# One power on GpSimd for both units of a step, the first tile's decoding behind it, and larger costs in the planner

## The chip, the cores and the metric

The kernel runs on one core of a Trainium2 chip. The core has a matrix engine (TensorE, PE in the rows), three engines for elementwise work (VectorE as DVE, ScalarE as ACT, GpSimd as POOL) and a queue engine (SyncE, SP) that issues most of the transfers. Each engine runs its own list of instructions in order and waits on semaphores for the others. The metric is the device time of one execution in microseconds, lower is better. It is compared with that of the kernel before on the same chip.

## The reference, cut to what matters

Three stages follow one another: a chunked linear-attention scan, a gated feed-forward layer behind an RMS norm, and a feed-forward layer with a squared ReLU.

```python
# scan, per chunk: M = (C B^T) * decay;  y = M x + (C state) * decay;  state = decay_full * state + sum(B x)
x = attn_out.transpose(0, 2, 1, 3).reshape(B * S, H * D)          # 3072 tokens of 256
rms = np.sqrt(np.mean(x * x, axis=-1, keepdims=True) + 1e-06)
xn = x / rms * rms_g
g = xn @ w_gate;  val = xn @ w_val                                # 256 -> 1536
x = (g * sigmoid(g) * val) @ w_out                                # 1536 -> 256
r = np.maximum(x @ w_in, 0.0)                                     # 256 -> 2048
out = (s * (r * r) + b) @ w_out2                                  # 2048 -> 256
```

The factor 1/rms is the part that the change touches: the kernel takes it as (mean of squares + 1e-6) to the power -0.5, on GpSimd.

## The kernel before

**The scan** goes in 16 steps of two *units* (`NPAIR = 2`, `NUNIT = 32`); a unit is one chunk of 48 positions of two batches. The stages of a step are `scan` (decay products `ab`, then a scan into `a_sb`), `gram` (64 small products `y<-raw_bc`, and the masks `m` from them on VectorE), `outs` (`y<-m,xh`, copied to `yt` by ScalarE), `back` (four transposes `y<-ident,yt` that put tokens on partitions, then the RMS norm) and `turn` (four transposes `y<-ident,xn` and the copies to `xth`, `xtl`, the input of the first layer). In `back`, for each unit: the state rows go to `xh` of the next step (`keep_state`), ScalarE squares the tokens with a running sum (`xn,ss<-y`, an ACTIVATE and a read of its accumulator), VectorE adds 1e-6 (`ss<-ss`), GpSimd takes the power (`rs<-ss,fixed`, a 128x1 tensor_tensor) and ScalarE scales the tokens (`xn<-y,rs`).

**The two layers** go over 8 blocks of 384 tokens, two steps each. The weights come as 64-bit floats and are decoded on the chip (`decode`: VectorE masks `e<-raw` and `raw<-raw`, ScalarE `e<-e` and `sg<-raw`, VectorE `w1f<-raw`, `e<-e,sg`, `w1f<-w1f,e`). Block 0 of layer 1 runs in halves of 192 columns with four-pass f32 products straight from `w1f` (`hidden1_plain`: four `h<-xth,w1f`, a SiLU on ScalarE, a product `h<-h,h` on VectorE, two `o<-h,w1f`), since the weights of tile m have only just been decoded. All later products are split into three one-pass products of a high and a low part, 384 columns each. Layers 1 and 2 of the blocks alternate, and the later scan steps are laid between their products.

**The order** on every engine is written by the class `Plan`, which records every operation and issues all of them from its method `issue` (one line, so every row of the trace has that line, L343 before and L349 now). It is a list scheduler: `price` gives the cost of an operation, `need` the delay from an operation to one that depends on it (a semaphore), `forward` and `backward` make the order from these. So a changed price moves instructions on all engines. `paced` operations are the products of the two layers; a *bundle* holds the products of one stage of both units of a step together, from unit 4 (`FREE`) on. Before `issue`, small bf16 products on constants are put in where the plan has TensorE idle at the start. `nc.after` makes the operations that follow wait, in the plan alone, for a recorded one.

Of the kernel before, what the change touches and what calls it, by code (L numbers as in the profile page):

```python
# [8 lines left out]
F32 = mybir.dt.float32  # L9
F32R = mybir.dt.float32r  # L10
# [6 lines left out]
AF = mybir.ActivationFunctionType  # L17
ALU = mybir.AluOpType

P = 128  # L20
# [8 lines left out]
NPAIR = 2  # L29
NUNIT = CPB * NPAIR  # L30
NCLIP = 2 * NPAIR
FREE = 2 * NPAIR
# [8 lines left out]
DM = 256  # L41
# [4 lines left out]
class Engine:  # L46
    def __init__(self, plan, name):
        self.plan, self.name = plan, name
# [5 lines left out]
class Plan:  # L54
# [16 lines left out]
    EARLY = 18.0  # L71
    STICK = 0.03
    SWITCH = {"matmul": 0.24, "transpose": 0.15}
    PASSES = 3

    def __init__(self, nc):
        self.nc, self.ops, self.clock, self.pace = nc, [], 0.0, False
        self.seen, self.rings, self.masks, self.before, self.heads = {}, {}, {}, {}, {}
        self.closed, self.sent, self.turns, self.bundle = set(), None, False, None
        self.fresh, self.after = False, None  # L80
        for e in ("tensor", "vector", "scalar", "gpsimd", "sync"):
            setattr(self, e, Engine(self, e))

    def add(self, eng, fn, args, kw):
# [21 lines left out]
        if self.fresh and op["eng"] == "tensor":  # L106
            op["dur"] += self.SWITCH[fn]
            self.fresh = False
# [72 lines left out]
    def need(self, op, o):  # L181
        if o is not op:
            lag = 0.0 if o["eng"] == op["eng"] == "tensor" else self.SEM_OF.get(o["eng"], self.SEM)
            op["preds"][o["i"]] = lag + (self.DMA_TAIL if o["fn"] == "dma_start" else 0.0)

    def price(self, eng, fn, args, kw):
        out = kw.get("out", args[0] if args else None)
        n = out.free_size()
        aps = [a for a in list(args) + list(kw.values()) if hasattr(a, "tensor")]
        psum = any("PSUM" in str(a.space) for a in aps)  # L190
        if fn == "dma_start":
            return max(0.06, out.nbytes() / self.DMA_RATE)
        if eng == "tensor":
            if fn == "transpose":
                return max(n / 1.2, 80) / 1e3 + 0.005
            w, four = kw["lhsT"], kw["lhsT"].dtype == F32
            cols = w.free_size()
            if w.ap[0][1] <= R:
                return 0.030 if w.ap[0][1] == NST else 0.014
            return max(4 * n / 2.4 + 5 if four else n / 2.285 + 7, (1.64 if four else 0.8) * cols) / 1e3  # L200
        if eng == "scalar":
            extra = 93 * sum(k in kw and hasattr(kw[k], "tensor") for k in ("scale", "bias"))
            extra += 230 if "accum_out" in kw else 120 if out.ap[0][1] < 32 else 0
            return (n / 1.2 + (60 if psum else 100) + extra) / 1e3
        if eng == "vector":
            sizes = [SIZE[a.dtype] for a in aps if a.free_size() > 1]
            fast = not psum and fn in ("tensor_scalar", "tensor_copy", "memset")
            fast = fast or (fn == "tensor_tensor" and not psum and max(sizes) == 2)
            more = 62 if fn == "scalar_tensor_tensor" and hasattr(kw["scalar"], "tensor") else 0
            if fn == "tensor_tensor_scan":  # L210
                n *= 2
            return (n / (1.92 if fast else 0.96) + 67 + more) / 1e3
        if fn == "tensor_tensor":
            return 0.7
        return n / 1.15e3 + (0.25 if fn == "affine_select" else 0.06)

    def lasts(self, op, now):
# [91 lines left out]
    def issue(self, idle, warm):  # L309
# [13 lines left out]
        found = []  # L323
        for _ in range(self.PASSES):
            start, stop = self.forward(succs, late)
# [31 lines left out]
def scan_glu_relu2(ctx: ExitStack, tc: tile.TileContext, bc, xr, aa, cst, w1, w2, gn, sv, bv, out):  # L357
    nc = Plan(tc.nc)
    PS = bass.MemoryType.PSUM

    const = ctx.enter_context(tc.tile_pool(name="const", bufs=1))
# [5 lines left out]
    att2 = ctx.enter_context(tc.tile_pool(name="att2", bufs=2))  # L367
# [17 lines left out]
    mhalf, emin = fixed[:, 0:1], fixed[:, 1:2]  # L385
    a_cl = const.tile([P, 4, R], F32, name="a_cl")
    warm = const.tile([P, 1], F32, name="warm")
    a_scr = dram.tile([2 * NUNIT, NH * AW], F32, name="a_scr")

    w1h = [wts.tile([P, 6, P], F32R, name=f"w1h{m}") for m in range(F1)]  # L390
# [6 lines left out]
    a_t, x_t, m_t, y_t, yt_t, xn_t = {}, {}, {}, {}, {}, {}  # L397
# [67 lines left out]
    def bundled(name, units, products):  # L465
        if units[0] >= FREE:
            nc.bundle = f"{name}{units[0]}"
        nc.fresh = True
        for c in units:
            products(c)  # L470
            nc.fresh = nc.fresh or units[0] < FREE
        nc.bundle = None
# [62 lines left out]
    def keep_state(c, tok):  # L535
        for z in range(2):
            rows = slice(z * R, z * R + NST)
            copy = nc.scalar.copy if c >= NPAIR else nc.vector.tensor_copy
            copy(out=x_t[c + NPAIR][rows], in_=tok[rows])

    def back(units):
        bundled("b", units, back_products)
        if units[0] == 0:
            nc.first_back = len(nc.ops) - 1
        for c in units:
            tok = y_t[c][:, 0, 0:DM]
            if c + NPAIR < NUNIT:
                keep_state(c, tok)
            xn = att2.tile([P, DM], F32, tag="xn", name="xn")
            ss = att2.tile([P, 1], F32, tag="ss", name="ss")  # L550
            nc.scalar.activation(out=xn, in_=tok, func=AF.Square, scale=DM ** -0.5, accum_out=ss)
            rs = att2.tile([P, 1], F32, tag="rs", name="rs")
            nc.vector.tensor_scalar(out=ss, in0=ss, scalar1=1e-6, scalar2=None, op0=ALU.add)
            nc.gpsimd.tensor_tensor(out=rs, in0=ss, in1=mhalf, op=ALU.pow)
            nc.scalar.activation(out=xn, in_=tok, func=AF.Copy, scale=rs)
            xn_t[c] = xn


    def columns(t, j):
# [30 lines left out]
    def stream():  # L590
        s = []
        for c in range(0, NUNIT, NPAIR):
            units = range(c, c + NPAIR)
            s += [(6 * c + t, units, f) for t, f in zip((2, 4, 8, 11, 14), (scan, gram, outs, back, turn))]
        s.sort(key=lambda e: e[0])
        return [(units, f) for _, units, f in s]


    def decode(raw, out, n):

        low = raw.bitcast(U32).rearrange("p (n w) -> p n w", w=2)[:, :, 0]
        high = raw.bitcast(I32).rearrange("p (n w) -> p n w", w=2)[:, :, 1]
        top_u = raw.bitcast(U16).rearrange("p (n w) -> p n w", w=4)[:, :, 3]
        top_i = raw.bitcast(I16).rearrange("p (n w) -> p n w", w=4)[:, :, 3]
        e = dec_p.tile([P, 6 * P], U16, tag="e", name="e")[:, :n]
        sg = dec_p.tile([P, 6 * P], BF16, tag="sg", name="sg")[:, :n]

        nc.vector.tensor_scalar(out=e, in0=top_u, scalar1=0x7FF0, scalar2=None, op0=ALU.bitwise_and)
        nc.scalar.activation(out=e, in_=e, func=AF.Relu, scale=8.0, bias=emin)
        nc.scalar.activation(out=sg, in_=top_i, func=AF.Sign)  # L610

        nc.vector.tensor_scalar(
            out=high, in0=high, scalar1=0xFFFFF, scalar2=0x100000,
            op0=ALU.bitwise_and, op1=ALU.bitwise_or,
        )
        nc.vector.scalar_tensor_tensor(
            out=out, in0=low, scalar=2.0 ** -32, in1=high, op0=ALU.mult, op1=ALU.add
        )
        pw = e.bitcast(BF16)
        nc.vector.tensor_tensor(out=pw, in0=pw, in1=sg, op=ALU.mult)  # L620
        nc.vector.tensor_tensor(out=out, in0=out, in1=pw, op=ALU.mult)

# [14 lines left out]
    def decode1(m):  # L637
        if m not in raw1:
            load1(m)
        raw = raw1.pop(m)  # L640
        w1f[m] = wlo.tile([P, 6, P], F32, tag="wlo", name="w1f")
        decode(raw, flat(w1f[m]), 6 * P)
# [10 lines left out]
    def decode2(m):  # L653
        raw = w2_p.tile([P, 4 * P], I64, tag="w2", name="raw2")
        words(raw, w2[m])
        w2f[m] = raw.bitcast(F32).rearrange("p (n w) -> p n w", w=2)[:, :, 1]
        decode(raw, w2f[m], 4 * P)
# [125 lines left out]
    def drain(n):  # L783
        while len(pending) > n:
# [4 lines left out]
                      in_=aa.rearrange("c (u f) -> (c u) f", u=2))  # L789
# [7 lines left out]
        out=ident, in_=ident, compare_op=ALU.not_equal, fill=1.0, base=0,  # L797
# [3 lines left out]
    for z in range(2):  # L801
        rows = slice(z * R, (z + 1) * R)
        nc.vector.tensor_copy(
            out=delta[rows, :, 0:CH], in_=ident[rows, None, z * R + NST:(z + 1) * R].to_broadcast([R, NH, CH])
        )
        nc.vector.memset(delta[z * R:z * R + NST, :, 0:1], 1.0)
    for u in range(4):
        rows = slice(u * 32, (u + 1) * 32)
        nc.vector.tensor_copy(
            out=raw_bc[rows, :, 0:NST], in_=ident[rows, None, u * 32:u * 32 + NST].to_broadcast([32, SLOTS, NST])  # L810
# [136 lines left out]
```

## Time and profile before

| | us |
|---|---|
| median of 3 runs | 668.23 |
| lowest and highest | 666.39, 670.76 |
| the profiled execution's own time | 669.25 |
| its span in the trace | 667.1 |
| TensorE busy in the span | 649.6 |
| VectorE busy | 385.2 |
| ScalarE busy | 361.4 |
| GpSimd busy | 36.0 |

The span is what the trace covers; the profiled execution took 2.15 us more than it. Busy times are sums over the span: an engine that is busy for half of it may still be the one that is waited for in one stretch.

### The profile page before, as it was taken

To read this page: it belongs to the slowest core of one execution; us is meant where nothing else is said; L and a number is where in the kernel's file an instruction comes from. 1 tells how busy PE (TensorE), PEld (TensorE's weight loads), DVE (VectorE), ACT (ScalarE), POOL (GpSimd) and SP (SyncE) were. 2 spreads that over 40 slices of the span, in tenths; PEclk is the share of its full clock that TensorE was granted. 3 is DMA by queue.
4 is the path that set the end of the run, shared out by engine and by line. 5 is a ranking of instruction groups with operands and counts; after the bars stand their busy time and mean duration, and the time that the engine had idled before them with its cause. 6 is when DMAs were issued, how large, how long until landed. Compare 5 with 4: busy or idle time off the path is not lost.

```text
span 667.1 us, 14004 instructions
## 1 busy us (share of the span) xinstructions
PE 649.6 (97%) x5575; PEld 629.8 (94%) x5575; DVE 385.2 (58%) x832; ACT 361.4 (54%) x814; POOL 36.0 (5%) x76
## 2 busy tenths in 40 slices
PE   6899999999999999999999999999999999999997
PEld 4699899899999999999999989999999999999997
DVE  6799999899644553355534464344633554344443
ACT  3688748876545663357534573346533565344453
POOL 3000200100000000001000010000000000000000
PEclk9699999999999999999999999999999999999999
DMA  7587660400001040003100030000400000000000
GB/s 216 183 250 267 199 240 13 93 1 0 1 2 25 23 96 13 0 2 84 46 0 1 14 93 25 1 1 13 93 25 0 1 3 25 0 1 1 11 13 25
DMA packets 26176, 35.06 MB, mean 53 GB/s; under 512 B 13696, under 2 KB 20480, under 8 KB 26112
## 3 DMA queue, kind: packets, MB, share of 16 engines
q1 hardware_dynamic: 25856, 33.98, 17.5%
q8 instruction: 44, 0.72, 0.4%
q10 hardware_dynamic: 256, 0.20, 0.1%
q14 instruction: 20, 0.16, 0.1%
HBM read 30.92 MB, written 3.25 MB: 51 GB/s over the span
## 4 chain that ended last, share of the span: by engine, by line
PE 87%; DVE 4%; ACT 3%; POOL 2%; issue 1%; DMA 1%; SPq 0%; DVEq 0%; POOLq 0%
PE h L343 48%; PE o L343 33%; PE y L343 6%; POOL rs L343 2%; ACT s L343 1%; DVE w1f L343 1%; DVE e L343 1%; DMA a_sb<-a_scr 1%; PE ab L343 1%; ACT xh L343 1%; DVE m L343 0%; DVE raw L343 0%; ACT xn L343 0%; ACT e L343 0%; DMA xh<-in_xr 0%
## 5 line engine op out<-in xcount | busy, mean ns | idle before, releaser
L343 ACT ACTIVATE s<-h 128x384 f32<-128x384 f32 x212 | 104.1, 491 | 152.5 <-PE h L343 110.3
L343 PE MATMUL h<-x,w2hl 128*128 128x384 f32 x768 | 165.4, 341 | 0.0
L343 DVE TENSOR_TENSOR lo<-s,hi 128x384 fp32r<-128x384 f32 x212 | 118.0, 556 | 48.3 <-ACT hi L343 37.3
L343 PEld LDWEIGHTS h<-x,w2hl 128*128 128x128 f32 x768 | 135.4, 188 | 1.1
L343 PE MATMUL o<-hi,w2hl 128*128 128x384 f32 (+1 forms) x512 | 133.0, 338 | 0.0
L343 PE MATMUL h<-xth,w1h 128*128 128x384 f32 x336 | 114.2, 340 | 0.3 <-ACT xth L343 0.3
L343 PE MATMUL h<-xtl,w1h 128*128 128x384 f32 x336 | 113.8, 340 | 0.0
L343 PE MATMUL h<-xth,w1l 128*128 128x384 f32 x336 | 113.5, 338 | 0.0
L343 DVE CAST hi<-s 128x384 fp32r<-128x384 f32 x128 | 46.0, 359 | 113.8 <-ACT s L343 103.2
L343 PEld LDWEIGHTS o<-hi,w2hl 128*128 128x128 f32 x512 | 93.2, 188 | 0.5
L343 DVE TENSOR_TENSOR s<-h,s 128x384 f32<-128x384 f32 x84 | 46.6, 555 | 78.0 <-PE h L343 78.0
L343 PE MATMUL o<-lo,w2hl 128*128 128x384 f32 (+1 forms) x256 | 86.6, 338 | 0.0
L343 ACT CAST hi<-s 128x384 fp32r<-128x384 f32 x84 | 43.1, 513 | 74.6 <-DVE s L343 74.4
L343 ACT ACTIVATE s<-s 128x384 f32<-128x384 f32 x128 | 67.3, 526 | 3.4
L343 PEld LDWEIGHTS h<-xth,w1h 128*128 128x128 f32 x336 | 63.1, 188 | 1.2 <-ACT xth L343 0.6
L343 PEld LDWEIGHTS h<-xtl,w1h 128*128 128x128 f32 x336 | 63.1, 188 | 0.5 <-DVE xtl L343 0.4
L343 PEld LDWEIGHTS h<-xth,w1l 128*128 128x128 f32 x336 | 63.1, 188 | 0.0
L343 PE MATMUL o<-hi,w1l 128*128 128x384 f32 x168 | 57.0, 339 | 0.0
L343 PE MATMUL o<-hi,w1h 128*128 128x384 f32 x168 | 56.9, 339 | 0.0
L343 PE MATMUL o<-lo,w1h 128*128 128x384 f32 x168 | 56.6, 337 | 0.0
L343 POOL TENSOR_TENSOR rs<-ss,fixed 128x1 f32<-128x1 f32 x32 | 30.6, 986 | 447.1 <-DVE ss L343 447.1
L343 PEld LDWEIGHTS o<-lo,w2hl 128*128 128x128 f32 x256 | 48.1, 188 | 0.0
(66 smaller groups left out, 698.2 us busy)
## 6 DMA issues: line engine op xcount, KB each, us to landing
raw<-in_w SPq DMA_DIRECT2D x12, 768.0 KB, 4.9
raw<-in_w SPq DMA_DIRECT2D x16, 512.0 KB, 5.8
a_sb<-a_scr SPq DMA_DIRECT2D x28, 196.0 KB, 4.1
raw_bc<-in_bc SPq DMA_DIRECT2D x64, 64.0 KB, 3.4
xh<-in_xr SPq DMA_DIRECT2D x60, 48.0 KB, 2.9
out_t<-ob SPq DMA_DIRECT2D x14, 192.0 KB, 2.5
out_t<-ob SPq DMA_DIRECT2D x4, 96.0 KB, 2.4
xh<-in_xr ACTq DMA_DIRECT2D x4, 48.0 KB, 3.6
```

The lines of the kernel that those rows point to most:

```text
L343: getattr(engine, op["fn"])(*op["args"], **op["kw"])
```

## The change

Of a step, both units' sums of squares now stand in one tile `ss` of two columns. One `ss<-ss` and one power `rs<-ss,fixed`, both 128x2, follow the squares of both units, where two of each stood before; the two `xn<-y,rs` come behind. In the first step the result of the power is copied on VectorE to a tile `held` that nothing reads, and the first tile's `w1f<-raw` is placed behind that copy in the plan; the first tile's `e<-e` on ScalarE is placed behind the squares. In the planner a power costs 0.9 us in steps below unit 4 and 2.0 us after (0.7 before), the products of a bundle count 0.6 us more on what they wait for on other engines, and a product of layer 1 counts 1.0 us more on `xth` and `xtl`.

```diff
+    LATE = 0.6
@@ def need
+            if op["eng"] == "tensor" != o["eng"] and self.bundle is not None:
+                lag += self.LATE
+            if op["paced"] and str(getattr(o["kw"].get("out"), "name", "")).startswith("xt") and op["kw"]["rhs"].dtype == F32R:
+                lag += 1.0
@@ def price
         if fn == "tensor_tensor":
-            return 0.7
+            return 0.9 if self.now_free else 2.0
@@ def back
+        ss = att2.tile([P, NPAIR], F32, tag="ss", name="ss")
...
-            xn = att2.tile([P, DM], F32, tag="xn", name="xn")
-            ss = att2.tile([P, 1], F32, tag="ss", name="ss")
-            nc.scalar.activation(out=xn, in_=tok, func=AF.Square, scale=DM ** -0.5, accum_out=ss)
-            rs = att2.tile([P, 1], F32, tag="rs", name="rs")
-            nc.vector.tensor_scalar(out=ss, in0=ss, scalar1=1e-6, scalar2=None, op0=ALU.add)
-            nc.gpsimd.tensor_tensor(out=rs, in0=ss, in1=mhalf, op=ALU.pow)
-            nc.scalar.activation(out=xn, in_=tok, func=AF.Copy, scale=rs)
-            xn_t[c] = xn
+            xn = xn_t[c] = att2.tile([P, DM], F32, tag="xn", name="xn")
+            nc.scalar.activation(
+                out=xn, in_=tok, func=AF.Square, scale=DM ** -0.5, accum_out=ss[:, c % NPAIR:c % NPAIR + 1]
+            )
+        if units[0] == 0:
+            nc.squares = len(nc.ops) - 1
+        rs = att2.tile([P, NPAIR], F32, tag="rs", name="rs")
+        nc.now_free = units[0] < FREE
+        nc.vector.tensor_scalar(out=ss, in0=ss, scalar1=1e-6, scalar2=None, op0=ALU.add)
+        nc.gpsimd.tensor_tensor(out=rs, in0=ss, in1=mhalf.to_broadcast([P, NPAIR]), op=ALU.pow)
+        if units[0] == 0:
+
+            nc.vector.tensor_copy(out=held, in_=rs)
+            nc.held = len(nc.ops) - 1
+        for c in units:
+            nc.scalar.activation(out=xn_t[c], in_=y_t[c][:, 0, 0:DM], func=AF.Copy, scale=rs[:, c % NPAIR:c % NPAIR + 1])
@@ def decode
+        nc.after = nc.squares
         nc.scalar.activation(out=e, in_=e, func=AF.Relu, scale=8.0, bias=emin)
+        nc.after = nc.squares = None
...
+        nc.after, nc.held = nc.held, None
         nc.vector.scalar_tensor_tensor(
             out=out, in0=low, scalar=2.0 ** -32, in1=high, op0=ALU.mult, op1=ALU.add
         )
```

VectorE at the first step's norm, before (`raw_125` is tile 0 of layer 1 and `raw_126` tile 1; in the rows now they are `raw_126` and `raw_127`; `xh<-y` copies out of PSUM):

```order
L343 TENSOR_SCALAR ss<-ss 128x1
L343 COPY xh<-y 16x256
L343 TENSOR_SCALAR ss<-ss 128x1
L343 SCALAR_TENSOR_TENSOR w1f<-raw_125 128x768
L343 TENSOR_TENSOR e<-e,sg 128x768
L343 TENSOR_SCALAR e<-raw_126 128x768
L343 TENSOR_TENSOR w1f<-w1f,e 128x768
L343 TENSOR_SCALAR raw_126<-raw_126 128x768
```

The same place now:

```order
L349 COPY xh<-y 16x256
L349 TENSOR_SCALAR ss<-ss 128x2
L349 COPY xh<-y 16x256
L349 TENSOR_SCALAR e<-raw_127 128x768
L349 TENSOR_TENSOR e<-e,sg 128x768
L349 COPY held<-rs 128x2
L349 SCALAR_TENSOR_TENSOR w1f<-raw_126 128x768
L349 TENSOR_TENSOR w1f<-w1f,e 128x768
L349 SCALAR_TENSOR_TENSOR a_sb<-ab,delta 128x392
L349 TENSOR_SCALAR raw_127<-raw_127 128x768
```

Behind `ss` VectorE had five operations of the decoding in a row; now two of them stand there, then the copy that waits for GpSimd, and the rest of tile 0 follows it.

TensorE behind the first step's norm, before (one row of `h` or `o` with 192 columns is two records in the trace, one row of `raw_bc` or `m,xh` too):

```order
L343 MATMUL y<-ident,xn 128x128 x4
L343 MATMUL h<-xth,w1f 128x192 x4
L343 MATMUL y<-raw_bc 64x64 x32
L343 MATMUL ab<-a_cl,ident 64x196 x4
L343 MATMUL h<-xth,w1f 128x192 x2
L343 MATMUL y<-m,xh 32x64 x16
```

The same place now:

```order
L349 MATMUL y<-ident,xn 128x128 x4
L349 MATMUL y<-raw_bc 64x64 x32
L349 MATMUL h<-xth,w1f 128x192 x4
L349 MATMUL y<-m,xh 32x64 x16
L349 MATMUL h<-xth,w1f 128x192
L349 MATMUL ab<-a_cl,ident 64x196 x4
```

The second step's `gram` moved ahead of the first products of layer 1. On the SyncE queue one load of `xh` also moved ahead of the last three of the four `raw_bc` loads that this `gram` reads.

ScalarE at the norm of a late step (the twelfth of sixteen), before:

```order
L343 ACTIVATE xn,ss<-y 128x256 x2
L343 COPY xh<-y 16x256 x2
L343 ACTIVATE xn<-y,rs 128x256
L343 ACTIVATE s<-h 128x384
L343 ACTIVATE xn<-y,rs 128x256
L343 ACTIVATE s<-s 128x384
L343 COPY xh<-y 16x256 x2
L343 ACTIVATE xth<-y,sb 128x2x48 x4
```

The same step now:

```order
L349 ACTIVATE xn,ss<-y 128x256 x2
L349 ACTIVATE s<-h 128x384
L349 COPY xh<-y 16x256
L349 ACTIVATE s<-s 128x384
L349 COPY xh<-y 16x256 x2
L349 ACTIVATE s<-h 128x384
L349 COPY xh<-y 16x256
L349 ACTIVATE xn<-y,rs 128x256 x2
```

All four state copies now stand ahead of the two scalings. On TensorE, between this step's transposes of `yt` and those of `xn`, stood 21 products of 384 columns, and now stand 33. At the third step it was 13 products of 192 columns and is 19; at the sixth 22 products of 384 columns, and now 32.

## Rows read from the trace of the kernel before

**Rows 1.** Part 1 of the page: busy us, share, instructions.

```profile
PE 649.6 (97%) x5575; PEld 629.8 (94%) x5575; DVE 385.2 (58%) x832; ACT 361.4 (54%) x814; POOL 36.0 (5%) x76
```

**Rows 2.** Waits of TensorE: us in total, times, longest.

```profile
PE y L343 <- ACT xn L343: 5.1, 2, 4.1
PE y L343 <- ACT xh L343: 3.1, 5, 1.5
```

**Rows 3.** Timeline of the first step: start, us, engine, operation, count, idle before.

```profile
11.91 4.43 POOL L343 TENSOR_TENSOR rs<-ss,fixed 128x1 f32<-128x1 f32 x2 [8.91 <-DVE ss L343]
12.19 0.94 DVE L343 SCALAR_TENSOR_TENSOR w1f<-raw 128x768 f32<-128x768 uint32 x1
13.05 0.54 DVE L343 TENSOR_TENSOR e<-e,sg 128x768 bf16<-128x768 bf16 x1
13.52 0.54 DVE L343 TENSOR_SCALAR e<-raw 128x768 uint16<-128x768 uint16 x1
...
14.86 0.54 DVE L343 TENSOR_SCALAR raw<-raw 128x768 int32<-128x768 int32 x1
15.85 0.99 ACT L343 ACTIVATE xn<-y,rs 128x256 f32<-128x256 f32 x2 [2.69 <-POOL rs L343]
16.38 1.21 PE L343 MATMUL y<-ident,xn 128*128 128x128 f32 x4 [4.08 <-ACT xn L343]
17.70 0.56 DVE L343 TENSOR_TENSOR e<-e,sg 128x768 bf16<-128x768 bf16 x1 [2.30 <-ACT e L343]
18.18 2.93 PE L343 MATMUL h<-xth,w1f 128*128 128x192 f32 x8 [0.59 <-ACT xth L343]
```

**Rows 4.** The tile `rs`: durations of its writers, ns, min/median/max.

```profile
L343 POOL TENSOR_TENSOR rs<-ss,fixed x32: 539/828/3908, 11.9 to 552.2; 128x1 f32<-128x1 f32 x32
```

**Rows 5.** Timeline at the sixth step's norm, VectorE, GpSimd and ScalarE.

```profile
123.79 0.55 DVE L343 TENSOR_TENSOR s<-h,s 128x384 f32<-128x384 f32 x1
123.95 3.20 POOL L343 TENSOR_TENSOR rs<-ss,fixed 128x1 f32<-128x1 f32 x2 [11.24 <-DVE ss L343]
124.81 0.48 ACT L343 ACTIVATE xn<-y,rs 128x256 f32<-128x256 f32 x1
...
126.66 0.55 DVE L343 TENSOR_TENSOR s<-h,s 128x384 f32<-128x384 f32 x1
127.18 0.47 ACT L343 ACTIVATE xn<-y,rs 128x256 f32<-128x256 f32 x1 [1.52 <-POOL rs L343]
```

**Rows 6.** Busy time by stretch: length, PE, PEld, DVE, ACT, POOL, clock, DMA share, GB/s.

```profile
15.40:33.60 18.20, 15.06 (x176) 11.40 (x176) 13.11 (x26) 11.76 (x25) 1.69 (x3) 0.72 0.63 200
12.30:37.00 24.70, 18.05 (x194) 13.72 (x193) 19.58 (x37) 16.02 (x37) 6.06 (x4) 0.79 0.68 204
37.00:130.00 93.00, 90.28 (x998) 86.03 (x998) 88.37 (x186) 68.67 (x157) 10.99 (x8) 1.00 0.55 180
```

**Rows 7.** The same view in stretches of 2 us, around the first transposes of `xn`.

```profile
14.00:16.00 2.00, 0.00 (x0) 0.00 (x0) 1.40 (x3) 0.15 (x1) 2.00 (x2) 1.00 0.87 278
...
18.00:20.00 2.00, 1.81 (x6) 1.82 (x7) 1.94 (x4) 1.31 (x4) 0.00 (x0) 0.50 0.52 191
```

**Rows 8.** The SyncE queue's `raw_bc` loads (timeline), and their time to landing (DMA view, 3 to 40 us).

```profile
10.40 1.96 SPq L343 DMA_DIRECT2D raw_bc<-in_bc  x3
...
raw_bc<-in_bc SPq DMA_DIRECT2D x13, 64.0 KB, 3.9
```

**Rows 9.** Timeline at the twelfth step's norm, GpSimd, ScalarE and TensorE.

```profile
393.97 2.08 POOL L343 TENSOR_TENSOR rs<-ss,fixed 128x1 f32<-128x1 f32 x2 [11.57 <-DVE ss L343]
396.87 0.72 ACT L343 COPY xh<-y 16x256 f32<-16x256 f32 x2
397.64 0.44 PE L343 MATMUL y<-ident,xn 128*128 128x128 f32 x2 [0.76 <-ACT xh L343]
```

**Rows 10.** Products at full clock: chain of work (384 columns), timeline (192 columns, two records each).

```profile
555.74 2.12 PE h L343 x12
...
33.63 1.57 PE L343 MATMUL h<-xth,w1f 128*128 128x192 f32 x8
```

More of the change, by code (lines that the diff above doesn't have):

```diff
@@ L79, in __init__ @@
         self.closed, self.sent, self.turns, self.bundle = set(), None, False, None
-        self.fresh, self.after = False, None
+        self.now_free = True
+        self.fresh, self.after, self.held, self.squares = False, None, None, None
         for e in ("tensor", "vector", "scalar", "gpsimd", "sync"):
@@ L387, in scan_glu_relu2 @@
     warm = const.tile([P, 1], F32, name="warm")
+    held = const.tile([P, NPAIR], F32, name="held")
     a_scr = dram.tile([2 * NUNIT, NH * AW], F32, name="a_scr")
@@ L619, in decode @@
         pw = e.bitcast(BF16)
+        nc.after = None
         nc.vector.tensor_tensor(out=pw, in0=pw, in1=sg, op=ALU.mult)
```

## The prediction

> **What bounds the kernel now.** I read busy times first. TensorE is busy for 649.6 of 667.1 us [rows 1], so 17.5 us is all that a change of order can win, apart from work done at a lower clock. Next, the waits of TensorE: it waited 5.1 us for `xn` (twice, once 4.1) and 3.1 us, in five places, for what ScalarE does around `xn` (`xh`) [rows 2]. Both stand at transposes `y<-ident,xn`, one step behind the power on GpSimd. Then the stretches [rows 6]: from 12.3 to 37 us TensorE is idle for 24.70 - 18.05 = 6.65 us, and from 37 to 130 for 93.00 - 90.28 = 2.72. In the later stretch VectorE is busy too, 88.37 of 93.
>
> The first step shows why [rows 3]. GpSimd's two powers take 4.43 us from 11.91. ScalarE scales at 15.85, TensorE transposes at 16.38 after 4.08 idle. The first power ends when VectorE has come to the end of its row of decoding (14.86 + 0.54 = 15.40). A power can take 539 ns, and this one, the longest, took 3908 [rows 4]. The sixth step says the same [rows 5]: the first power started while VectorE ran `s<-h,s`, with one operand in PSUM, and was done by 124.81; the second was done at 123.95 + 3.20 = 127.15, half a microsecond after VectorE came to the next such operation (126.66). So a power waits while VectorE works on SBUF operands back to back.
>
> The Trainium skill has this as a rule: GPSIMD Engine Reference, section Specifications, says that GpSimd shares its SBUF interfaces with VectorE and contends with instructions in a two-port mode or with two SBUF inputs. The trace agrees (3908 against 539 ns).
>
> The idle time has a second price. The clock stood at 1.00 from 14 to 16 us, while TensorE had nothing to do, and at 0.50 (1.2 of 2.4 GHz) from 18 to 20 [rows 7]. The mean of 0.79 over 24.7 us [rows 6] makes 2 x 0.21 x 24.7 = 10.4 us at the lower level. There, eight records of `h` took 2.93 us [rows 3], against 1.57 at full clock [rows 10].
>
> **Term A, the first step.** The removed power is nothing by itself; what counts is when the remaining one ends. `ss` now follows both squares and is finished near 11.9 (before, the two stood at 11.6 and 12.1), so the power starts near 12.0. VectorE then runs `xh<-y` out of PSUM until about 12.3, `e<-raw` and `e<-e,sg` (0.54 each, overlapping a little, until 13.25), and stops at `held`. Lower bound of the power's end: 12.0 + 0.82 = 12.8, as the first power of the sixth step (123.95 to just before 124.81), which also met an open VectorE first. Upper bound: it gets nothing until VectorE stops, 13.25 + 0.45 = 13.7. That it has two columns instead of one is shown by no row; I take it as inside these bounds. I take 13.2, midway, since its open time is shorter than in that row. Before, the end was 15.82, so the scaling and the transposes come 2.6 us earlier, at 13.75.
>
> By the skill's rule the two operations ahead of `held` (one in a two-port mode, one with two SBUF inputs) still shut the power out, and the end would be 13.7; the sum below would then be 0.5 higher.
>
> What `held` costs: behind it on VectorE wait the rest of tile 0 (two operations of 0.94), the second step's scan and all decoding, and for these the products `h`. VectorE stands from 13.25 to 13.3 at best, 13.8 at worst. Before, it did that work in this time, but then stood 2.30 us for ScalarE's `e`, which was queued behind the waiting `xn` [rows 3]; that wait goes. Between 15.4 and 33.6 us VectorE is busy for 13.11 of 18.20 us [rows 6], so it had 5.09 us to give. The list of operations up to the second step's `ss` is the same but for one `ss` fewer and `held`, so that `ss` can come up to 5.1 us earlier.
>
> What is late next: the second step's `gram` now stands ahead of `h`. Three of its `raw_bc` loads were issued from 10.40 on, the last near 11.3, and a load lands 3.9 later (median) [rows 8], near 15.2; one `xh` load now goes first, 0.4 more. TensorE therefore stands from 14.4 to about 15.6, and `h` starts near 16.6 instead of 18.18, with `gram` already done. The masks `m` and tile 1 then come from VectorE, which is the pace.
>
> If the clock stays up, A is what VectorE gives, up to 5.1. If it falls, TensorE does the same work at half rate until about 27, and A is the earlier transposes (2.6) and the wait of 0.59 behind them, near 3.2. With 1.5 and 1.2 us of idle time instead of 4.08 I take the clock to stay up more often than not, and **A = 4.5** (3 to 5.1).
>
> The clock bears on the skill too: TensorE: Matmul & The Clock Gate, section What's actually happening, calls the lower level the default, which activity lifts. The fall to 0.50 behind the 4.08 us agrees. No row says on which side 1.5 and 1.2 fall.
>
> **Term B, later waits.** From 37 us on, the waits at `xn` are 5.1 - 4.1 = 1.0 and 3.1, together 4.1 us. The twelfth step shows one [rows 9]: powers 2.08 us from 393.97, then two `xh` at 396.87, and the transposes go on at 397.64 after 0.76. The planner had counted 0.7 for a power; it now counts 2.0 and 0.6 more for the bundle. So 33 products of 384 columns stand where 21 stood. A product is 2.12 / 12 = 0.177 us [rows 10], so TensorE arrives 2.1 us later, and all four `xh` come before the scaling. The third step has six more products of 192 columns (1.57 / 4 = 0.39 each, 2.3 us), the sixth ten more of 384 (1.8 us). Each is more than its wait (1.5 at most). Against it: both scalings now need the one power, which starts behind the second square. Price of a power, from both sides: 0.54 alone, some 2.4 for the second of the sixth step (124.8 to 127.15). At 2.4 the first scaling is as late as the second was, and the second 0.5 later. That is inside the 1.8 to 2.3 us, if nothing else on ScalarE has moved ahead. All goes at best, 1.5 at worst; I take **B = 3.0**.
>
> **Term C, VectorE.** A and the part of B before 130 (1.5 + 1.0) move TensorE up by some 7 us there. VectorE moves up by A, and has 93.00 - 88.37 = 4.6 us idle for the rest. The new order asks for some scans and masks earlier. I put down **0.3 us lost**, between 0 and 3. Fifteen other `ss` of 0.13 fewer win nothing that can be seen. The larger delay before `xth` (1.0) only adds distance: what fills it is other products.
>
> **The sum.** 669.25 - 4.5 - 3.0 + 0.3 = 662.05 against the profiled execution's time. The median of the runs is 1.02 lower than that execution, so 661.0, 1.1% below 668.23.
>
> **Rivals.** (1) *The clock falls all the same.* A is 3.2: 662.3 to 663. For it: TensorE's work between 12 and 16 us is small and broken by two waits. (2) *Clock stays and VectorE never limits:* 5.1 + 4.1, and a power that ends at 12.8: 658.6. (3) *The later waits stay*, with a power that starts later and is still shut out by VectorE's scans: B = 0.5, so 663.5. Against it, the counted products. (4) *The first power is slow by itself* (a first use), not by VectorE. Then it ends at 15.8 again, VectorE stands for 2.5 us at `held`, loses what it had before the old stall, A is 0 and B is 3: 665.2. Against it: the end 0.42 behind VectorE's last operation, and the sixth step. (5) *Slower: VectorE becomes the bound between 40 and 85 us.* The 24 half tiles of block 0 each need a `h<-h,h` and a decoded tile. If scans and masks, now earlier, make each of the 24 groups wait 0.4 us, 9.6 us are lost: 670.6. It decides from the point where these waits exceed A + B = 7.5, that is 0.31 us per group. For it: 88.37 of 93 us busy; against it, 4.6 idle, and TensorE kept 97% of that stretch.
>
> **How the numbers follow.** Chances: the forecast 0.45 (660 to 662.3), (1) 0.17, (2) 0.13, (3) 0.12, (4) 0.07, (5) 0.06. A measurement of this kernel tells about 1% from no change, that is 661.5. Below it lie most of the forecast's cases, say 0.30, all of (2) and little of (1) and (3): 0.46. Above 674.9 lies nothing named but the far end of (5); for that, or an order that goes wrong in a place that I did not walk through, 0.04. The rest, 0.50, is within 1%. The range reaches from (2) with a little more on the clock, 657.5, to beyond (4), 666.5; (5) is left out.
>
> **What would show it.** In the changed profile: the first power ends between 12.8 and 13.7 and lasts 0.8 to 1.7 us; the first `y<-ident,xn` starts near 13.8; TensorE waits there about 1.5 us and then for `raw_bc`; the clock either stays at 1.00 from 16 to 27 us or not; the second step's `ss` stands near 28 to 29; waits `<-ACT xn` and `<-ACT xh` together fall from 8.2 us to about 2.5; TensorE's idle time from 37 to 130 is under 2 us. Wrong would be: a first power near 3.9 us again (rival 4), or new waits of TensorE for `w1f`, `h` or `m` between 40 and 130 us (rival 5).

## The result, and the profile after

The changed kernel took 661.11 us (median of 4 runs, 660.66 to 661.66), the kernel before 669.5 beside it (four runs, 666.39 to 671.91): a ratio of 0.9878, 95% interval 0.9832 to 0.9923. More rounds on another chip (e12 below) gave 0.987, 0.9839 to 0.9901. The forecast was 661.0. The profiled execution took 660.78 us, 8.47 less than that of before; the sum had 7.2.

Part 1 of its page, against [rows 1]:

```profile
span 658.7 us, 13932 instructions
...
PE 646.5 (98%) x5575; PEld 630.7 (96%) x5575; DVE 384.0 (58%) x817; ACT 360.2 (55%) x814; POOL 20.8 (3%) x60
```

TensorE's idle time fell from 17.5 to 12.2 us, 5.3 less; its busy time fell too, by 3.1, though it has the same 5575 instructions. So not all of the gain is to be found among the waits. These are now, against [rows 2]:

```profile
PE y L349 <- ACT xn L349: 1.8, 1, 1.8
PE y L349 <- DVE m L349: 1.8, 2, 1.0
PE y L349 <- ACT yt L349: 1.2, 2, 0.7
PE y L349 <- ACT xth L349: 0.8, 1, 0.8
```

One wait for `xn` is left and none for `xh`: 8.2 us have become 1.8. The timeline of the first step, and the second step's norm, against [rows 3]:

```profile
12.10 0.90 POOL L349 TENSOR_TENSOR rs<-ss,fixed 128x2 f32<-128x2 f32 x1 [9.10 <-DVE ss L349]
13.35 0.16 DVE L349 COPY held<-rs 128x2 f32<-128x2 f32 x1
13.56 0.81 PE L349 MATMUL y<-ident,xn 128*128 128x128 f32 x4 [1.83 <-ACT xn L349]
15.21 3.08 PE L349 MATMUL y<-raw_bc 16*64 16x64 f32 x64 [0.85 <-ACT xth L349]
18.22 2.93 PE L349 MATMUL h<-xth,w1f 128*128 128x192 f32 x8
29.36 0.15 DVE L349 TENSOR_SCALAR ss<-ss 128x2 f32<-128x2 f32 x1
35.68 1.16 PE L349 MATMUL y<-raw_bc 16*64 16x64 f32 x64
```

The transposes come 2.8 us earlier. But the second step's `gram` behind them takes 3.08 us where the same 64 products take 1.16 at 35.68, so that the first `h` starts at 18.22, as before (18.18). The stretches give most of the reason, in the columns of [rows 6] and [rows 7]:

```profile
12.30:37.00 24.70, 20.60 (x265) 17.55 (x266) 21.75 (x40) 17.91 (x41) 2.88 (x2) 0.79 0.95 249
37.00:130.00 93.00, 92.33 (x957) 89.06 (x957) 92.08 (x193) 70.74 (x164) 5.45 (x4) 1.00 0.51 168
...
14.00:16.00 2.00, 1.15 (x13) 0.79 (x14) 1.93 (x3) 2.00 (x6) 0.00 (x0) 0.68 0.91 221
16.00:18.00 2.00, 2.00 (x58) 2.00 (x56) 2.00 (x4) 0.34 (x1) 0.00 (x0) 0.50 1.01 373
...
28.00:30.00 2.00, 2.00 (x8) 2.00 (x9) 2.00 (x5) 1.98 (x5) 0.40 (x1) 0.59 1.04 182
```

The clock fell all the same, and again near 28 us, behind waits of 1.00, 0.55 and 0.45 us in the timeline. The mean of 0.79 over 24.7 us is that of before. In the kernel before the 64 products of this `gram` took 2.46 us at a clock of 0.50 (from 21.04); what the other 0.6 of the 3.08 us went into was not traced. VectorE is busy for 21.75 + 92.08 = 113.83 us from 12.3 to 130 us; before it was 19.58 + 88.37 = 107.95. With the same work to do (384.0 us in all, 385.2 before) it is 5.9 us further at 130 us.

The powers, against [rows 4] (durations in ns, min/median/max):

```profile
L349 POOL TENSOR_TENSOR rs<-ss,fixed x16: 690/692/2207, 12.1 to 540.2; 128x2 f32<-128x2 f32 x16
```

The same view of the forty transposes of `xn` from 130 us on (before: 270/272/332, with four waits of TensorE for `xh`, 1.7 us):

```profile
L349 PE MATMUL y<-ident,xn x40: 270/272/273, 217.6 to 545.0; 128*128 128x128 f32 x40
```

Timed from its first start to the start of the next product, each of these ten sets of four now takes 0.35 or 0.36 us, 3.55 in all. Before, six took as much and four, broken by a wait, 0.81, 0.99, 1.34 and 0.81: 6.09 in all. That makes 2.5 us. At 130 us the products of the two layers are 5.5 us ahead of before, and the whole span is 8.4 us shorter, so these two places hold most of the gain.

### The profile page after: what moved, and what is told of

Same layout as the page of the kernel before. It is cut to its first block, busy times and chain, and to the rows that moved or that the text cites. A ratio compares the mean times of both kernels' runs of the same rounds, so it can differ in the third digit from the quotient of the medians.

```text
span 658.7 us, 13932 instructions
## 1 busy us (share of the span) xinstructions
PE 646.5 (98%) x5575; PEld 630.7 (96%) x5575; DVE 384.0 (58%) x817; ACT 360.2 (55%) x814; POOL 20.8 (3%) x60
## 4 chain that ended last, share of the span: by engine, by line
PE 92%; DVE 4%; DMA 2%; ACT 1%; issue 1%; SPq 0%; DVEq 0%
PE h L349 51%; PE o L349 35%; PE y L349 6%; DVE raw L349 1%; DMA raw<-in_w 1%; DVE e L349 1%; DMA xh<-in_xr 1%; DVE s L349 0%; DMA raw_bc<-in_bc 0%; DVE xtl L349 0%; DVE lo L349 0%; DVE w2hl L349 0%; DVE w1f L349 0%; DVE m L349 0%; ACT xth L349 0%
## 5 line engine op out<-in xcount | busy, mean ns | idle before, releaser
L349 PE MATMUL h<-x,w2hl 128*128 128x384 f32 x768 | 162.4, 340 | 0.0
L349 PE MATMUL h<-xth,w1f 128*128 128x192 f32 x192 | 39.0, 346 | 1.0 <-ACT h L349 0.5
```

Source lines behind the costliest of these rows:

```text
L349: getattr(engine, op["fn"])(*op["args"], **op["kw"])
```

## The experiments

Each was run with the kernel before on the same chip; a ratio is to that.

| kernel | us (median) | ratio | 95% interval |
|---|---|---|---|
| e1, change with before's numbers | 671.04 | 1.0018 | 1.0002 to 1.0034 |
| e2, two powers, new numbers | 663.01 | 0.9904 | 0.9877 to 0.9931 |
| e3, change without `held` | 665.17 | 0.9929 | 0.9902 to 0.9956 |
| e4, more filling products | 660.82 | 0.9872 | 0.9848 to 0.9896 |
| e5, filling ahead of `xn` | 660.91 | 0.9863 | 0.9840 to 0.9886 |
| e6, power's price only | 660.53 | 0.9862 | 0.9840 to 0.9885 |
| e7, delays only | 664.60 | 0.9922 | 0.9906 to 0.9938 |
| e8, two powers, price only | 667.50 | 0.9956 | 0.9938 to 0.9975 |
| e9, two powers, delays only | 661.91 | 0.9849 | 0.9816 to 0.9881 |
| e10, power's price 4.0 | 662.23 | 0.9858 | 0.9830 to 0.9886 |
| e11, eight operations cut | 660.33 | 0.9827 | 0.9798 to 0.9856 |
| e12, the change again | 661.31 | 0.9870 | 0.9839 to 0.9901 |

### The one power without the numbers, and the numbers without it (e1, e2)

```diff
-    LATE = 0.6
+    LATE = 0.0
-                lag += 1.0
+                lag += 0.0
-            return 0.9 if self.now_free else 2.0
+            return 0.7
```

> The code of the change with the planner's old numbers: a power costs 0.7 us, a bundle no 0.6 more, the products of layer 1 no 1.0 more on xth. My theory (the power of the first step wins about 2.7 us, the planner's numbers win the later waits, about 5.6): 666 to 667 us, the first power still near 0.9 us, waits of TensorE at the transposes of xn of 2.5 us or more in sum after 37 us. Rival (one power in place of two removes the later waits by itself): 661 to 663 us, those waits under 1 us.

```diff
+            return 0.45 if self.now_free else 1.0
```

(in the kernel before with its two powers, and with both delays)

> The code of the kernel before (a power for each unit, no held) with the planner's new numbers, half a price for each of the two powers (0.45 and 1.0 us), so that both cost what the one costs in the change. My theory: the later waits go and the first step stays as it was: 663 to 665 us, first power 3 to 4 us, waits at the transposes of xn after 37 us under 1 us. Rival (the numbers win nothing without the single power, since two powers in a row behind a busy VectorE still come late): 667 to 669 us.

The one power by itself (e1) won nothing: 671.04. Both times of its expectation were missed; the waits that its theory named came (from 37 us on 3.0 us for `xn` and 1.1 for `xh`). Its first step came out as planned (power of 0.85 us, transposes at 14.76), and at the 65th product of the layers (here and below, the 65th record of `h` or `o` in the trace) it was 1.5 us ahead of before. It lost that at the fifth and the sixth step (powers of 2.94 and 3.14 us). The timeline of the sixth:

```profile
123.73 0.41 DVE L349 TENSOR_TENSOR e<-e,sg 128x512 bf16<-128x512 bf16 x1
123.89 3.14 POOL L349 TENSOR_TENSOR rs<-ss,fixed 128x2 f32<-128x2 f32 x1 [11.10 <-DVE ss L349]
...
125.80 0.68 DVE L349 TENSOR_TENSOR raw<-raw,e 128x512 f32<-128x512 f32 x1
127.07 0.84 ACT L349 ACTIVATE xn<-y,rs 128x256 f32<-128x256 f32 x2 [2.17 <-POOL rs L349]
127.59 0.80 PE L349 MATMUL y<-ident,xn 128*128 128x128 f32 x4 [1.77 <-ACT xn L349]
...
128.32 0.56 DVE L349 TENSOR_TENSOR s<-h,s 128x384 f32<-128x384 f32 x1 [1.84 <-ACT s L349]
```

VectorE's row of decoding holds the power until it ends (125.80 + 0.68 = 126.48); ScalarE waits for the power, so its next SiLU waits too, and VectorE stands 1.84 us for that. The clock fell behind TensorE's wait of 1.77 us, in stretches of 2 us:

```profile
128.00:130.00 2.00, 1.86 (x10) 1.54 (x10) 1.53 (x4) 2.00 (x7) 0.00 (x0) 0.79 0.20 45
130.00:132.00 2.00, 2.00 (x8) 2.00 (x7) 2.00 (x7) 1.36 (x4) 0.00 (x0) 0.50 0.00 0
```

A power for both units makes both wait for the later square, and the `xn` transposes still stood 20 to 22 products behind `yt`. Two powers with the new numbers (26 to 28 behind, from the seventh step on) took 663.01, so most of the gain comes without the one power. Its theory had the first step as before, and missed that: the first transposes of e2 came at 12.78.

### What `held` does (e3)

```diff
-        if units[0] == 0:
-
-            nc.vector.tensor_copy(out=held, in_=rs)
-            nc.held = len(nc.ops) - 1
-        nc.after, nc.held = nc.held, None
```

> The change without the copy to held and without what it holds back: VectorE goes on decoding tile 0 while the first power runs. My theory (a power is shut out while VectorE works on SBUF operands back to back): the first power takes 2.5 to 4 us again and the time is 663 to 665 us. Rival (the first power is short because it is one with two columns, and held only makes VectorE wait): first power under 1.3 us, 660 to 661 us.

Timeline of its first step:

```profile
13.14 3.99 POOL L349 TENSOR_TENSOR rs<-ss,fixed 128x2 f32<-128x2 f32 x1 [10.14 <-DVE ss L349]
...
15.15 0.94 DVE L349 SCALAR_TENSOR_TENSOR w1f<-raw 128x768 f32<-128x768 uint32 x1
16.02 0.54 DVE L349 TENSOR_TENSOR e<-e,sg 128x768 bf16<-128x768 bf16 x1
17.17 0.84 ACT L349 ACTIVATE xn<-y,rs 128x256 f32<-128x256 f32 x2 [2.78 <-POOL rs L349]
17.70 0.90 PE L349 MATMUL y<-ident,xn 128*128 128x128 f32 x3 [4.51 <-ACT xn L349]
```

The first power is shut out again, 3.99 us, until 0.57 us behind VectorE's last operation. Beside the 0.90 us of the change, that settles the fourth rival: it was never a slow first use. In e1 and e7 the power starts in the middle of the same `e<-raw` as here, and with `held` behind `e<-e,sg` it took 0.85 us in both. The time, 665.17, is just above the theory's 663 to 665, and 4.1 above the change. It is the middle of two groups: three runs with a mean granted clock of 0.993 or 0.994 took 663.18 to 663.95 us, three with 0.990 took 666.38 to 666.97.

### Clock or VectorE in the first step (e4, e5, e11)

```diff
-    SPARE = 1.2
+    SPARE = 0.1
```

> The change with more of the small products on constants in the idle time of TensorE at the start (the planner leaves 0.1 us free ahead of the next product instead of 1.2). My theory for the first step (it won 2.7 instead of 4.5 us because the clock fell all the same): granted clock 1.00 from 12 to 28 us and 658.5 to 660 us. Rival (VectorE sets the pace there, so the clock is worth nothing): clock 1.00 and 660.5 to 662 us.

```diff
-                while busy + self.FILL + self.SPARE < start[i]:
+                spare = 0.1 if op["fn"] == "transpose" and op["args"][1].name.startswith("xn") else self.SPARE
+                while busy + self.FILL + spare < start[i]:
```

> The change, with 26 filling products in place of 6 ahead of the first two xn transposes; the other waits get no more than the change gives them. Theory: the clock stays at full speed from 12 to 28 us because the 1.83 us of idle time at 13.56 is gone, the first power still ends near 13.0, and the first step gives back what separates the forecast's first term of 4.5 us from the measured 2.7, so 659.0 to 659.8 us. Rival: VectorE sets the pace of the first steps whatever the clock is, so the lead shows only until about 40 us and the time is that of the change, 660.5 to 662 us.

In e4 the clock stayed at 1.00 from 12 to 37 us, and the time did not move. That is no clean test of the clock's price: the filling also delayed the first `y<-m,xh` (9.37, in the change 7.67) and the first transposes of `xn` (15.54; 13.56). Yet the 65th product stood at 38.40 (38.82). The stretch from 12.3 us of e4:

```profile
12.30:37.00 24.70, 20.46 (x323) 16.73 (x320) 23.50 (x44) 19.92 (x45) 2.93 (x2) 1.00 0.91 222
```

And what VectorE waited for there, up to 60 us:

```profile
DVE e L349 <- DMA raw<-in_w: 1.2, 1, 1.2
```

VectorE is busy for 95% of the stretch (in the change 88%), and then waits for a load of weights. In e5's profiled run the first step was no test: ScalarE reached the scaling late, since a load of weights came at 13.49, the wait of 1.62 us at `xn` stayed, and the clock fell. Its four runs are one, though: two with a mean granted clock of 0.991 and 0.997 took 661.33 and 661.34 us, two with 1.000 and 0.999 took 660.48 and 660.39. So the clock is worth some 0.9 us here, as seen across four runs. e4 says much the same: four runs with 0.999 or 1.000 have a median of 660.26, two with 0.995 and 0.997 took 661.26 and 661.49.

The kernel before pays more. Of its nineteen runs beside e1 to e4, seven with a mean granted clock of 0.995 have a median of 668.27 us, and five with 0.988 to 0.990 one of 671.26. These spent some 7.5 us more at the lower level (2 x 0.0056 x 670), and 3 us go with that. Where they are lost is open, since one profile of that kernel was kept.

```diff
+        cut = 16 if nc.signs <= 8 else n
-        nc.vector.tensor_tensor(out=pw, in0=pw, in1=sg, op=ALU.mult)
+        nc.vector.tensor_tensor(out=pw[:, :cut], in0=pw[:, :cut], in1=sg[:, :cut], op=ALU.mult)
```

> The change in the same order on every engine; the product with the signs is made for 16 of 768 columns in the first eight decoded tiles of layer 1, so these weights lose their signs, and VectorE does eight operations of about 0.1 us in place of eight of 0.55 us before 60 us. Theory: VectorE sets the pace from 16 to 60 us, whatever the clock does; then most of the 3.6 us shows as an earlier block 0 and 657.5 to 659 us. Rival: the lower clock (10.24 us of it) or the chain of the first step sets it; then less than 1 us comes off, 660 to 661.5 us.

With 3.1 us less for VectorE to do (eight times 0.16 in place of 0.55) in the same order, the 33rd to the 113th product came 0.75 to 1.0 us earlier than in the change. Then a load was late (VectorE's timeline), TensorE waited for what it decodes (TensorE's), and from the 137th product on nothing of the lead was left:

```profile
39.25 0.56 DVE L349 TENSOR_SCALAR e<-raw 128x768 uint16<-128x768 uint16 x1 [0.85 <-DMA raw<-in_w]
...
48.95 1.54 PE L349 MATMUL h<-xth,w1f 128*128 128x192 f32 x8 [0.36 <-DVE w1f L349]
```

Its profiled span was 659.1 us, the change's 658.7, and its median of 660.33 lies in the rival's range. The ratios leave the size of a gain open: 0.9827 is below the change's 0.987, the intervals overlap by little, and the change was not run on that chip. What the two traces show is that VectorE is the pace at first, and that the loads of weights are right behind it.

### Which number covers the later waits (e6 to e10)

e6 sets both delays to 0.0 in the change; e7 keeps them and puts the power's price back to 0.7; e10 makes the price 4.0. e8 and e9 are the kernel before, with two powers: e8 with a price of 1.0 each after the free steps, e9 with both delays alone.

> The change with the two added delays taken out (products that the scan's products wait for), the power's higher price of 2.0 kept. Theory: the price of the power is what puts the xn transposes 28 to 30 products behind yt in place of 21 to 22, and that is enough to cover the power in most steps: 661 to 663.5 us, no wait of over 1 us at xn after 37 us. Rival: the delays are needed as well; then waits at xn come back and the time is 667 us or more.

> The change with the old price of 0.7 for the power, the two added delays kept: the xn transposes stand 23 to 25 products behind yt. Theory: about half of the cover, so waits at xn stay where VectorE shuts the power out (some of the places of 68, 113 and 127 us that the change with all the old numbers showed), 664 to 667 us. Rival: the delays do the work of the price too and the time is that of the change, 660.5 to 662 us.

> The kernel before with its two powers, and one number changed: 1.0 in place of 0.7 for each power after the free steps. The xn transposes then stand 23 to 29 products behind yt in place of 21 to 22, and the first step is as it was. Theory: only the broken sets of xn transposes go, without the first step's gain and without the delays, 665 to 667 us. Rival: the one number gives most of the gain of the change, 663 us or less.

> The kernel before with its two powers at 0.7 each, and the two added delays alone. The xn transposes stand 23 to 26 products behind yt (before 21 to 22; 23 to 29 with the power's price alone, which gave 667.5 us and left waits for xtl). Theory: the delays take away the waits for xtl and most of those at xn, so what the planner's numbers win with two powers (663.0 us with all of them) is mostly theirs: 663.5 to 666 us. Rival: it is the two together that cover a late power; alone the delays give no more than the price alone did, 667 us or more.

> The change with a power priced at 4.0 in place of 2.0 after the free steps; the xn transposes stand 42 to 44 products behind yt in place of 31 to 33. Theory: the waits at xn are gone already at 2.0, so a longer distance wins nothing: 660 to 662 us, and more only where a later xth makes a layer product wait. Rival: the sets are still broken by waits shorter than the profile lists, and the time falls below 659.5 us.

What TensorE waited for from 37 us on: in e6 the view lists nothing; in the change a SiLU and a product `s`, 0.7 us in all. In e7:

```profile
PE y L349 <- ACT xh L349: 1.4, 5, 0.3
PE h L349 <- ACT s L349: 0.6, 1, 0.6
```

In e8:

```profile
PE h L344 <- DVE xtl L344: 4.4, 4, 1.9
PE h L344 <- ACT s L344: 0.4, 1, 0.4
```

In e9:

```profile
PE h L349 <- ACT s L349: 0.6, 1, 0.6
```

In e10, the largest:

```profile
PE o L349 <- DVE lo L349: 1.2, 2, 0.7
```

e6 came out half a microsecond under its theory's range, at 660.53: with one power, the price alone gives all of it. Its profiled execution, the slowest of its five (663.08), had its first transposes only at 16.14, behind a load of weights that ScalarE had stood 2.50 us for. e7 held its theory's time; its waits are short ones for `xh`, and the broken sets are back: its ten sets of transposes take 5.46 us.

e8 came out half a microsecond above its theory's range, at 667.50, and for another reason than was written: the ten sets of transposes are whole (3.54 us), but the layer products wait 4.4 us for `xtl`. That is not because the transposes are late. In all four places VectorE has a scan ahead of `xtl`, and the scan stood 0.54 to 2.67 us for a load, three times `a_sb<-a_scr` and once `xh`. The longest, from VectorE's and TensorE's timelines:

```profile
475.19 0.97 DVE L344 TENSOR_TENSOR_SCAN a_sb<-a_sb,delta 128x392 f32<-128x392 f32 x1 [2.67 <-DMA a_sb<-a_scr]
476.08 0.97 DVE L344 SCALAR_TENSOR_TENSOR xtl<-y,sb,xth 128x96 fp32r<-128x96 f32 x4
476.66 0.45 PE L344 MATMUL h<-xtl,w1h 128*128 128x384 f32 x1 [1.90 <-DVE xtl L344]
```

Before and in e9 the scan stands ahead of `xtl` in four places too, but waited there 0.96 and 0.83 us at most. Why it stood longer in e8 was not tried.

Both the theory and the rival of e9 fell: with two powers the delays alone gave 661.91 and the ratio of the change. At much the same distance (23 to 26 products in e9, 23 to 25 in e7) two powers thus did better than one. e10, at 662.23, is 0.2 above its theory's range and far from its rival: past the point where the waits are gone, distance wins nothing.

e9 and e8 showed something else. Their first step is short with two powers too. This is e9's:

```profile
10.89 0.95 DVE L349 SCALAR_TENSOR_TENSOR w1f<-raw 128x768 f32<-128x768 uint32 x1
11.13 1.65 POOL L349 TENSOR_TENSOR rs<-ss,fixed 128x1 f32<-128x1 f32 x2 [8.13 <-DVE ss L349]
...
11.82 0.55 DVE L349 TENSOR_SCALAR e<-raw 128x768 uint16<-128x768 uint16 x1
12.29 0.55 DVE L349 TENSOR_TENSOR e<-e,sg 128x768 bf16<-128x768 bf16 x1
12.44 0.47 ACT L349 ACTIVATE xn<-y,rs 128x256 f32<-128x256 f32 x1
12.97 0.44 PE L349 MATMUL y<-ident,xn 128*128 128x128 f32 x2 [1.44 <-ACT xn L349]
```

The planner placed `w1f<-raw` ahead of the second `ss` in place of behind it, and the first transposes came at 12.97, earlier than in the change. That this placement is the cause was not tried apart.

### The change again (e12)

> The change itself once more, in more rounds, since two powers with the two delays alone came to a ratio of 0.9849 and the change to 0.9878 with an interval of 0.9832 to 0.9923. Theory: once the waits are covered the two are the same, a ratio between 0.984 and 0.988. Rival: the one power is still worth 2 us or more, a ratio of 0.982 or less.

A ratio of 0.987: the theory held, and no gain of one power over two is seen. Its profile also tells how far two executions of one program lie apart: the first `y<-m,xh` came at 8.15 in place of 7.67, the 65th product was 2.0 us ahead of before in place of 2.7, and a wait of 0.71 us for `lo` stands at 314.43, which the first profile doesn't have.

## Why the prediction came out as it did

**What it had right.** The end of the first power (13.00, foretold 12.8 to 13.7), its duration (0.90; 0.8 to 1.7), the first transposes (13.56; 13.8), the waits for `xn` and `xh` (1.8; 2.5), the idle time of TensorE from 37 to 130 us (0.67; under 2). The second step's `ss` was a little late (29.36; 28 to 29), and the wait behind the transposes was 0.85 us and is put down to `xth`, not to `raw_bc`. The mechanism, a power that VectorE shuts out, is shown by e3 and by e1's sixth step. It is not the whole rule: in the change the power was done at 13.00, and `e<-e,sg` ran until 12.88 + 0.55 = 13.43, so the power did not have to wait until VectorE stops, as the upper bound of 13.7 had it.

**Term A was too large.** It was 4.5. Counted in products of the layers, the 65th is 2.7 us ahead (38.82 against 41.49), in the second profile 2.0. The step that failed is "I take the clock to stay up more often than not": it fell behind idle times of 1.83 and 0.85 us, `gram` took 3.08 in place of 1.16, and `h` started at 18.22, not near 16.6. That is the first rival, at a price (3.2) not far off. The reason under it was wrong in part as well. "If the clock stays up, A is what VectorE gives, up to 5.1" left out the loads of weights. In e4 the clock stayed up, and the time was that of the change, though with a first step that began late; the runs of e5 put the clock at 0.9 us, not 1.3. What stands behind VectorE is the next `raw`, 1.2 us late in e4 and 0.85 in e11. Part of the 2.7 is no merit of the change at all: the first `y<-m,xh` came at 7.67 where before had 8.45, and that differs by half a microsecond between two executions.

**Term B was too small.** It was 3.0, and 4.1 at best. The last product of the layers is 8.35 us ahead, so 5.7 came behind the 65th; in the second profile it is 6.3 ahead, and 4.3 came there. All the waits went, not most. And a wait in the middle of a set costs more than its idle time: the four broken sets before took 2.5 us more than whole ones, of which the waits account for 1.7, which leaves 0.2 for each. That is 0.8 of the 3.1 us by which TensorE's busy time fell; the rest was not traced.

**Term C** was not seen: TensorE is busy for 99% of 37 to 130 us with VectorE at 99%. The fifth rival (VectorE the bound, 670.6) needed waits of 0.31 us in each of 24 groups; there is one of 0.5.

**The sum.** The two errors, 1.8 too much and 2.7 too little (by the second profile 2.5 and 1.3), had opposite signs. Against the profiled execution the sum said 662.05, and the run took 660.78. The median of before then came out at 669.5 with a fourth run, 1.27 above the first three. The agreement of 661.0 and 661.11 is therefore closer than the working deserves.

**What the prediction did not ask** is which part does it. It gave A to the one power with its `held`, and B to the numbers. The runs show that the numbers alone can do it: two powers with the delays reach the ratio of the change (0.9849 against 0.987), and one power without the numbers wins nothing (1.0018). `held` is worth its 4 us only with the one power (e3); with two, the delays gave a short first step without it (e9). The one power needs its price, since it ties the first unit to the second; with the price it needs no delays (e6).

**What stays open:** when GpSimd gets through. [Rows 3], e1 and e3 show powers that end 0.4 to 0.6 us behind the end of VectorE's row. In the change a power ended 0.43 us ahead of that, and in e9 one took 1.28 us and ended at 12.41 while VectorE worked from one SBUF operand to the next without a pause, a small `ss<-ss` (128x1) among them. The Trainium skill (GPSIMD Engine Reference, Specifications) says that instructions in a two-port mode or with two SBUF inputs contend; e3 agrees, and the powers of the change and of e9, which got through beside operations of the same kinds, are not explained by it. Which operation let it in was not tried.

## What to carry to other kernels

Where a planner sets the order, try the change of its numbers apart from the change of the work: here a delay of some products ahead of a late result did what merging two operations was given credit for. When a price is raised to cover a wait, look at every engine's order again: in e8 that wait went, and products came to wait for `xtl`, which stood behind a scan whose load was late. Before a shorter chain at the start is counted in full, ask which load is next: a lead that outruns the loads is given back at the first of them.

## What the runs showed of the hardware that was not expected

- The clock fell behind short idle times: 1.83 and 0.85 us in the first step, and in e1 a single wait of 1.77 us, which ended at 127.59, was followed by 0.50 from 130 to 132 us, with TensorE busy before and after. The Trainium skill (TensorE: Matmul & The Clock Gate, What's actually happening) calls the lower level the default, which activity lifts; the runs agree in that TensorE had stood idle ahead of each of these falls. In the kernel before a wait of 1.47 us, which ended at 70.59, was followed by no fall, so the length of a wait alone does not tell.
- With the change, ten microseconds at half clock cost about one (e5, four runs), in stretches where VectorE and the loads set the pace. In the kernel before, 7.5 us went with 3.
- A power on two columns takes 0.69 us by itself, on one 0.54 [rows 4]: two columns cost 0.15 more, not twice as much.
